# An attention and two-MoE kernel on one Trainium2 core: loads of v and of encoded weights in 64-row halves, k one slot sooner, decoding in other slots

## Chip, core and metric

The kernel runs on one core of one Trainium2 chip. The metric is the device time of one execution in microseconds (us). An execution with the profiler on gives the trace from which the rows below are read.

## The reference

For 4 batches, 12 heads, 448 tokens and 64 features per head the reference computes

```
scores = q @ k^T / 8                          (per batch and head, 448 x 448)
scores = sum over h of scores[h] * w_pre[h,g]
attn   = softmax(scores)
attn   = sum over h of attn[h] * w_post[h,g]
x      = attn @ v                             -> 1792 tokens x 768
x      = elu(x @ w_in) @ w_out                w_in 768 x 2048, w_out 2048 x 768
y      = top-1 mixture of 8 experts on x (768 -> 1024 -> 768, relu, gated)
```

w_in and w_out reach the kernel as 64-bit floats, seen as pairs of 32-bit words. The kernel makes 32-bit floats of them with a few integer steps, which it calls decoding.

## The kernel before

**Slots.** The attention stage walks through 16 chunks of queries (four per batch: 120, 120, 120 and 88 rows). A chunk is cut into units: six in each of the first three chunks of a batch, five in the last (four full ones and a half one). One unit is handled per *slot*; slots are numbered 0 to 91 in `S0`, 23 to a batch: 0 to 22, 23 to 45, 46 to 68, 69 to 91. The order of all instructions of all engines is written by hand: `at(slot, order, fn, ...)` files a call under a slot and a place in it, `half(y, ...)` under half slot y (slot y/2), and the calls run sorted by slot and order. The function `room` chooses between neighbouring half slots by a table of planned DVE and ACT costs.

**A unit.** The product of q and k (`qk`, L228) is copied from PSUM into the tile `st` by DVE and ACT (`qk_out`). Three slots ahead of a unit, `relayout` (L245) issues from POOL's queue the DMAs `sp<-st`, SBUF to SBUF, which bring the 12 heads of five queries into one column of partitions: four of 60 rows for a full unit. `premix` (L255) multiplies by w_pre, `rowmax` and `expo` (L261, L267) make the exponentials, `postmix` (L286) multiplies by w_post and the sums' reciprocals, `mt_out` (L304) copies the result. `av` (L332) multiplies by v once a chunk is complete, and `av_out` (L339, L340) sends the result to DRAM (`xscr`). The tile `sp` has 4 buffers, `ks` 9 (6 per batch), `raw` 2, `vt` 2.

**Loads.** All loads go from SP's queue, which takes them in the written order and stops at each that must wait:

- `load_q`: 192 KB, two per chunk. `load_k`: 224 KB, six per batch, for the next batch.
- `load_v` (L306 to L313): row blocks j = 0 to 3 of v at slots 1, 3, 5 and 7 of a batch (2, 4, 6 and 8 in batch 0). Blocks 0 to 2 are 128 rows of 3 KB in one DMA; block 3 has 64 rows, and they are loaded twice, into both halves of the partitions. In batch 0 each waits for a `premix` by `after(...)`.
- `dec_load` (L342): half a block of encoded weights, 128 rows of 3 KB.

**Decoding in the attention stage.** `dec_jobs` are three blocks of w_in and three of w_out, each in two halves: 12 half blocks. `spots` (L410) gives the slot of each one's first step: slots 10, 17 and 21 of batches 0 to 2, and slots 4, 8 and 13 of batch 3. The load is issued 5 half slots before. `dec_step` runs five DVE steps and one ACT step, and sends 128 rows of 1.5 KB of result to DRAM (`wscr`, `oscr`).

After the attention stage come the first MoE and the second one, which the change does not touch.

Of the kernel before, what the change touches and what calls it, by code (L numbers as in the profile page):

```python
# [8 lines left out]
U32 = mybir.dt.uint32  # L9
# [6 lines left out]
NB, H, S, D = 4, 12, 448, 64  # L16
# [84 lines left out]
def after(tc, ins, writes):  # L101
    for w in writes:
        tc.add_manual_dep(ins.ins, w.ins.name, mybir.DependencyInfo(mybir.DependencyClass.Sync, mybir.DependencyReason.DATA),
                          reason="rows of any scatter")
# [43 lines left out]
S0 = [0]  # L148
# [6 lines left out]
def attention(tc, pools, at, q, k, v, kron_pre, kron_post, dec_jobs, xscr):  # L155
# [3 lines left out]
    nc = tc.nc  # L159
    mm = nc.tensor.matmul  # L160
    sb = pools.open("a_sb", "right")
    early = pools.open("a_early", "left")
# [14 lines left out]
    dec = Decoder(nc, early, DM // 2, 2, 2, 2)  # L177

    ks, qs, qp, st, sp, pre, mxs, pt, sms, kpt, pst, mt, vt, avp, draw, dsteps, begun = ({} for _ in range(17))
# [5 lines left out]
    def values(b):  # L185
        vt[b] = sb.tile([128, 4, H, D], F32, name="vt", tag="vt", bufs=2)
# [116 lines left out]
        dst = mt[cc][:, :, 20 * g:20 * g + 2 * nr * T].rearrange("p x (w i) -> p w x i", i=T)  # L303
        nc.scalar.activation(dst, src, AF.Copy)  # L304

    def load_v(b, j):  # L306
        if j == 0 and b:
            values(b)
        n = min(128, S - 128 * j)
        for o in range(0, 128, n):  # L310
            ins = nc.sync.dma_start(vt[b][o:o + n, j], v[b, 128 * j:128 * j + n])
            if not b:
                after(tc, ins, [begun[divmod(1 + 2 * j, 6)]])  # L313

    def av(cc, a):

# [22 lines left out]
        nc.vector.tensor_copy(x[:, :, :n], avp.pop((cc, a))[:, :, :n])  # L339
        nc.sync.dma_start(xscr[b][:, 2 * a:2 * a + 2, o:o + n], x[:, :, :n])  # L340

    def dec_load(n, hf):  # L342
        draw[n, hf] = dec.load(dec_jobs[n][0], hf)

    def dec_step(n, hf, ix):
        if ix == 0:
            dsteps[n, hf] = dec.steps(draw.pop((n, hf)))
        fns, dst = dsteps[n, hf]
        fns[ix]()
        if ix == 5:  # L350
            nc.sync.dma_start(dec_jobs[n][1][:, hf * dec.width:(hf + 1) * dec.width], dst)
# [4 lines left out]
    def half(y, order, fn, *args):  # L356
        at(y / 2, order, fn, *args)
# [6 lines left out]
    def room(lo, hi, **cost):  # L364
        return take(min(range(lo, max(lo, hi) + 1), key=lambda y: max(use.get((e, y), 0) + c for e, c in cost.items())), **cost)

    def when(cc, u):

        if cc == 0:
            return 2 * ((2 * u + 1) * 10 // 12 - 13)  # L370
        lo, hi = S0[cc - 1] - 3, S0[cc] - 3
        return 2 * lo + u * (2 * hi - 2 * lo) // 6

    at(-100, 0, warm)
    for cc in range(NCH):
        z = S0[cc]
        for u in range(6):
            y = when(cc, u)
# [21 lines left out]
        half(y if soon else room(y + 1, y + 2, dve=35), 36, av_out, cc, a)  # L400
    for b in range(NB):
        for j in range(4):
            at(S0[4 * b] + 1 + 2 * j if b else 2 + 2 * j, 4, load_v, b, j)
        for u in range(6):
            half(when(4 * b, u) - 8 if b else 2 * (u - 20), 3, load_k, b, u)
    for cc in range(NCH):
        for u in range(2):
            half(when(cc, 3 * u) - 8 if cc else (-40, -36)[u], 3, load_q, cc, u)
    N = 2 * len(dec_jobs)
    spots = [S0[4 * b] + d for b in range(NB) for d in ((4, 8, 13) if b == NB - 1 else (10, 17, 21))]  # L410
    assert len(spots) == N
    first, free = 3, [0, 0]
    for i in range(N):
        n, hf = divmod(i, 2)
        z = max(first, free[i % 2], 2 * spots[i])
        first = y = room(z, z + 1, dve=85)
        half(y - 5, 3, dec_load, n, hf)
        half(y, 43, dec_step, n, hf, 0)
        half(y, 43, dec_step, n, hf, 2)
        y = room(y + 1, y + 2, act=61)  # L420
        half(y, 36, dec_step, n, hf, 1)
        y = room(y, y + 1, dve=57)
        half(y, 42, dec_step, n, hf, 3)
        y = room(y + 1, y + 2, dve=101)
        half(y, 43, dec_step, n, hf, 4)
        half(y, 43, dec_step, n, hf, 5)
        free[i % 2] = y + 1
# [934 lines left out]
def whole(tc, q, k, v, kron_pre, kron_post, w_in, w_out, w_gate, w1, w2,  # L1362
# [7 lines left out]
    with tc.tile_pool(name="dram", bufs=1, space=DRAM) as dr, tc.tile_pool(name="one", bufs=1, side="left") as one:  # L1370
# [17 lines left out]
        with tc.manual_schedule():  # L1388
            attention(tc, pools, at, q, k, v, kron_pre, kron_post,
                      [(src[f], to[f]) for src, to in ((w_in, wscr), (w_out, oscr)) for f in range(PRE)], xscr)  # L1390
            before, moe2_rest = moe2(tc, pools, w1, w2, ident, x2rows, R, out)
            moe1_rest = moe1(tc, pools, at, w_in, w_out, w_gate,
                             {"ident": ident, "tri": tri, "ones": ones, "em8": em8, "iota": iota, "tid": tid},
                             xscr, wscr, oscr, x2rows, R, before)
            for key in sorted(events):
                for fn, args in events[key]:
                    fn(*args)
            moe1_rest()
            moe2_rest()
# [61 lines left out]
```

## Time and profile before

| | |
|---|---|
| time before, median of 3 runs | 1202.42 us (1199.22 to 1205.14) |
| profiled execution, its own time | 1201.08 us |
| span of its trace (first to last instruction) | 1199.3 us |
| PE, DVE, ACT, POOL busy, share of the span | 96%, 64%, 57%, 25% |
| mean granted TensorE clock | 0.992 |

The time of the profiled execution is the span and 1.8 us around it. Engines: PE is TensorE's matmul, PEld its weight load, DVE VectorE, ACT ScalarE, POOL GpSimd, SP SyncE (it only issues DMAs here). An "idle before" is the time for which an engine stood idle just ahead of an instruction, with what ended it; "issue" is an engine that waited for nothing that the profile shows.

### The profile page before, as it was taken

What the parts mean: (1) busy time and instruction counts of PE and PEld (TensorE: products, weight loads), DVE (VectorE), ACT (ScalarE), POOL (GpSimd) and SP (SyncE); (2) the same over time, 40 slices, a digit from 0 to 9 for tenths busy, and PEclk for the clock granted to TensorE, in tenths of its full rate; (3) what the DMA queues carried; (4) which work ended last, traced back from release to release, by engine and by line L of the source; (5) the groups of instructions that cost most, each with busy time, mean ns of one, the idle gap of its engine ahead of it and who ended that gap; (6) DMA issues with size and microseconds to landing.
All of it is one profiled execution on the core that took longest, in us unless ns stands there. A gap on an engine that the chain in (4) does not pass through costs nothing.

```text
span 1199.3 us, 31078 instructions
## 1 busy us (share of the span) xinstructions
PE 1149.0 (96%) x12802; PEld 981.3 (82%) x12802; DVE 766.8 (64%) x1541; ACT 685.7 (57%) x1310; POOL 295.1 (25%) x466
## 2 busy tenths in 40 slices
PE   7989999899999999999999999999989999999995
PEld 3556666666667999999999987889779999999995
DVE  4667777667765878777777656555365655566662
ACT  4767777767776674645655344555434544455552
POOL 5656656546530003020211100000010110111110
PEclk9999999999999999999999999999999999999998
DMA  6997887888764428455573623334166665566551
GB/s 185 200 210 213 207 205 205 197 193 213 197 190 138 151 92 207 130 133 142 137 200 91 162 68 100 130 101 140 46 228 211 214 175 195 198 225 232 203 195 61
DMA packets 116444, 201.47 MB, mean 168 GB/s; under 512 B 45024, under 2 KB 76370, under 8 KB 116292
## 3 DMA queue, kind: packets, MB, share of 16 engines
q1 hardware_dynamic: 78116, 138.01, 37.1%
q0 software_dynamic: 38176, 61.37, 21.8%
q8 instruction: 103, 1.69, 0.6%
q14 instruction: 49, 0.40, 0.1%
HBM read 120.94 MB, written 30.09 MB: 126 GB/s over the span
## 4 chain that ended last, share of the span: by engine, by line
PE 85%; DMA 4%; ACT 3%; DVE 3%; issue 2%; POOL 1%; SPq 0%; POOLq 0%; ACTq 0%; DVEq 0%
PE p_h L533 14%; PE p_o L573 14%; PE p_h L1231 11%; PE p_z L1216 8%; PE p_post L286 7%; PE p_av L332 6%; PE p_qk L228 5%; PE p_pre L255 5%; PE acc L599 5%; PE p_o L533 4%; PE p_y L1231 3%; DMA sp<-st 3%; PE p_t L90 1%; POOL sp L245 1%; ACT mt L304 1%
## 5 line engine op out<-in xcount | busy, mean ns | idle before, releaser
L245 POOL DMA_DIRECT2D sp<-st x360 | 208.3, 593 | 135.4 <-PE p_pre L255 62.0
L267 ACT ACTIVATE pt<-p_pre,mx 128x448 f32<-128x448 f32 x180 | 112.9, 634 | 39.6 <-DVE mx L261 39.3
L286 PEld LDWEIGHTS p_post<-kp,pt 60*64 60x64 f32 (+1 forms) x5056 | 90.9, 135 | 43.7 <-ACT mt L304 26.3
L304 ACT ACTIVATE mt<-p_post 128x960 f32<-128x960 f32 (+1 forms) x92 | 101.6, 1104 | 42.1 <-PE p_post L286 42.0
L286 PE MATMUL p_post<-kp,pt 60*64 60x60 f32 (+2 forms) x5056 | 110.9, 229 | 11.3 <-issue 8.1
L261 DVE TENSOR_REDUCE mx<-p_pre 128x1 f32<-128x448 f32 x180 | 104.3, 619 | 23.2 <-PE p_pre L255 19.3
L590 POOL DMA_DIRECT2D x<-part x46 | 41.6, 928 | 291.5 <-ACT part L589 288.5
L1231 PE MATMUL p_h<-xgh,w1h 128*128 128x256 f32 (+1 forms) x384 | 109.6, 285 | 0.2 <-DVE h2l L1234 0.2
L1231 PE MATMUL p_h<-xgl,w1h 128*128 128x256 f32 (+1 forms) x384 | 109.3, 285 | 0.3 <-DVE xgl L1195 0.2
L1231 PE MATMUL p_h<-xgh,w1l 128*128 128x256 f32 (+1 forms) x384 | 109.3, 285 | 0.3 <-DVE w1l L112 0.3
L255 PE MATMUL p_pre<-sp,kpre 60*64 60x448 f32 x720 | 105.9, 540 | 3.3 <-DMA sp<-st 3.3
L573 PE MATMUL p_o<-gh,woh 128*128 128x448 f32 x288 | 106.4, 370 | 2.6 <-DVE x L586 2.6
L332 PEld LDWEIGHTS p_av<-mt,vt 128*64 128x64 f32 x1536 | 74.8, 137 | 38.9 <-issue 12.9
L573 PE MATMUL p_o<-gl,woh 128*128 128x448 f32 x288 | 105.2, 365 | 0.0
L573 PE MATMUL p_o<-gh,wol 128*128 128x448 f32 x288 | 104.9, 364 | 0.0
L228 PE MATMUL p_qk<-ks,qs 64*64 64x448 f32 x744 | 98.0, 541 | 5.0 <-ACT st L237 3.7
L235 DVE COPY st<-p_qk 128x448 f32<-128x448 f32 x93 | 57.9, 622 | 69.4 <-PE p_qk L228 56.3
L112 DVE TENSOR_TENSOR w2l<-w2raw,w2h 128x768 fp32r<-128x768 f32 (+1 forms) x60 | 60.7, 1012 | 51.4 <-ACT w2h L110 51.4
L332 PE MATMUL p_av<-mt,vt 128*64 128x120 f32 (+1 forms) x1536 | 85.6, 264 | 7.0 <-issue 5.1
L553 DVE SCALAR_TENSOR_TENSOR th<-rm,th 128x448 f32<-128x448 f32 x64 | 40.0, 625 | 80.6 <-ACT rm L552 80.6
L1267 POOL DMA_INDIRECT out_dram<-yrow,put x18 | 23.8, 1323 | 253.4 <-ACT w1h L110 86.7
L112 DVE TENSOR_TENSOR w1l<-w1raw,w1h 128x768 fp32r<-128x768 f32 x64 | 61.0, 960 | 28.2 <-ACT w1h L110 24.6
(199 smaller groups left out, 2811.6 us busy)
## 6 DMA issues: line engine op xcount, KB each, us to landing
sp<-st POOLq DMA_DIRECT2D x352, 105.0 KB
w1raw<-in_w_dram SPq DMA_DIRECT2D x64, 384.0 KB, 7.1
w2raw<-in_w_dram SPq DMA_DIRECT2D x48, 384.0 KB, 2.8
x<-part POOLq DMA_DIRECT2D x46, 224.0 KB
raw<-in_w_in_dram SPq DMA_DIRECT2D x13, 768.0 KB, 6.2
raw<-in_w_out_dram SPq DMA_DIRECT2D x13, 768.0 KB, 4.9
wtmp<-wscr SPq DMA_DIRECT2D x19, 384.0 KB, 3.9
wtmp<-oscr SPq DMA_DIRECT2D x19, 384.0 KB, 5.3
```

The lines of the kernel that those rows point to most:

```text
L112: nc.vector.tensor_tensor(l, src, a.bitcast(F32), ALU.subtract)
L228: mm(p[e][64 * a:64 * a + 64, :S], lhsT=qq[r, c:c + 64], rhs=kk[r], start=True, stop=True)
L245: nc.gpsimd.dma_start(t[64 * r:64 * r + 12 * T, c], st[cc][f:f + d * (T - 1) + 1:d])
L255: first = mm(ban[r][64 * c:64 * c + 64, :S], lhsT=kpre[x], rhs=t[x, c, :], start=True, stop=True)
L261: nc.vector.tensor_reduce(mxs[cc, g][:, r:r + 1], pre[cc, g][r][:, :S], AX.X, ALU.min)
L267: nc.scalar.activation(pt[cc, g][:, r], pre[cc, g][r][:, :S], AF.Exp, bias=mxs[cc, g][:, r:r + 1], scale=-1.0, accum_out=sms[cc, g][:, r:r ...
L286: mm(out, lhsT=e[x, r, 64 * s:64 * s + 64], rhs=kp[x, w].rearrange("p w (h i) -> p w h i", i=5)[:, :, :, :T], start=True, stop=True)
L304: nc.scalar.activation(dst, src, AF.Copy)
L332: mm(p[64 * e:64 * e + 64, u, :n], lhsT=vt[cc // 4][:, j, h, :], rhs=mt[cc][:, j * H + h, :n], start=(j == 0), stop=(j == 3))
L533: mm(p[:, :S], lhsT=a[:, c], rhs=m, start=(i == 0), stop=(i == 17))
L573: mm(p[:, :S], lhsT=a[:, c], rhs=m, start=(k == 0), stop=(k == 3 * len(fs) - 1))
L1231: mm(q[:, :N], lhsT=a[:, kk, :], rhs=m[:, kk, :], start=(j == 0), stop=(j == len(seq) - 1))
```

## The change

The loads of v become eight of 64 rows per batch, one per slot, in slots 0 to 7 of the batch (1 to 8 in batch 0, each behind the `premix` of the slot before). The loads of encoded half blocks become two of 64 rows, 6 and 5 half slots ahead of the decoding. k of the next batch is loaded two half slots (one slot) sooner. The 12 half blocks are decoded 2, 3, 3 and 4 per batch, not 3, 3, 3 and 3, in other slots.

```diff
-    def load_v(b, j):
-        if j == 0 and b:
+    def load_v(b, j, o):
+        if j == 0 and o == 0 and b:
             values(b)
-        n = min(128, S - 128 * j)
-        for o in range(0, 128, n):
-            ins = nc.sync.dma_start(vt[b][o:o + n, j], v[b, 128 * j:128 * j + n])
-            if not b:
-                after(tc, ins, [begun[divmod(1 + 2 * j, 6)]])
+        i = 128 * j + (o if j < 3 else 0)
+        ins = nc.sync.dma_start(vt[b][o:o + 64, j], v[b, i:i + 64])
+        if not b:
+            after(tc, ins, [begun[divmod(2 * j + o // 64, 6)]])
...
-    def dec_load(n, hf):
-        draw[n, hf] = dec.load(dec_jobs[n][0], hf)
+    def dec_load(n, hf, o):
+        w = 2 * dec.width
+        if o == 0:
+            draw[n, hf] = early.tile([128, w], U32, name="raw", tag="raw", bufs=2)
+        nc.sync.dma_start(draw[n, hf][o:o + 64], dec_jobs[n][0].bitcast(U32)[o:o + 64, hf * w:(hf + 1) * w])
...
         for j in range(4):
-            at(S0[4 * b] + 1 + 2 * j if b else 2 + 2 * j, 4, load_v, b, j)
+            for o in (0, 64):
+                at(S0[4 * b] + (0 if b else 1) + 2 * j + o // 64, 4, load_v, b, j, o)
         for u in range(6):
-            half(when(4 * b, u) - 8 if b else 2 * (u - 20), 3, load_k, b, u)
+            half(when(4 * b, u) - 10 if b else 2 * (u - 20), 3, load_k, b, u)
...
-    spots = [S0[4 * b] + d for b in range(NB) for d in ((4, 8, 13) if b == NB - 1 else (10, 17, 21))]
+    spots = [S0[4 * b] + d for b in range(NB) for d in ((3, 7, 11, 14) if b == NB - 1 else (11, 19, 22) if b else (19, 22))]
...
-        half(y - 5, 3, dec_load, n, hf)
+        half(y - 6, 3, dec_load, n, hf, 0)
+        half(y - 5, 3, dec_load, n, hf, 64)
```

## Rows read from the trace of the kernel before

**Rows 1.** The page: span, queue of instructions, chain that ended last.

```profile
span 1199.3 us, 31078 instructions
...
q8 instruction: 103, 1.69, 0.6%
...
PE 85%; DMA 4%; ACT 3%; DVE 3%; issue 2%; POOL 1%; SPq 0%; POOLq 0%; ACTq 0%; DVEq 0%
```

**Rows 2.** Windows of the attention, cut at slot starts: length, busy, clock, DMA, GB/s.

```profile
53.49:103.16 49.67, 46.34 (x1137) 31.59 (x1133) 36.15 (x96) 37.40 (x81) 31.29 (x55) 1.00 0.84 205
...
103.16:131.78 28.62, 28.62 (x717) 19.55 (x713) 20.43 (x57) 22.20 (x50) 19.28 (x34) 1.00 0.82 216
131.78:142.86 11.08, 10.32 (x252) 7.36 (x248) 6.89 (x18) 7.55 (x17) 5.93 (x11) 1.00 0.85 192
142.86:188.44 45.58, 43.41 (x1064) 29.70 (x1062) 33.91 (x92) 35.33 (x77) 26.91 (x48) 1.00 0.86 205
...
216.74:230.29 13.55, 10.41 (x252) 7.32 (x248) 6.89 (x18) 7.71 (x17) 6.72 (x12) 1.00 0.70 167
230.29:277.69 47.40, 44.76 (x1064) 30.75 (x1062) 34.04 (x92) 35.35 (x77) 26.80 (x48) 0.96 0.82 197
277.69:331.42 53.73, 49.91 (x1245) 34.52 (x1240) 39.73 (x108) 40.10 (x88) 33.52 (x59) 1.00 0.84 209
```

**Rows 3.** PE's timeline, first product of slots 43, 44 and 45: start, us.

```profile
179.12 0.98 PE L255 MATMUL p_pre<-sp,kpre 60*64 60x448 f32 x8
...
181.53 1.06 PE L255 MATMUL p_pre<-sp,kpre 60*64 60x448 f32 x8
...
186.03 0.97 PE L255 MATMUL p_pre<-sp,kpre 48*64 48x448 f32 x4
```

**Rows 4.** Windows with the DMA engines full, columns as in Rows 2.

```profile
154.29:166.00 11.71, 10.91 (x262) 7.04 (x258) 7.99 (x21) 8.56 (x20) 8.09 (x15) 1.00 1.07 232
...
237.23:252.31 15.08, 14.09 (x356) 9.41 (x352) 10.72 (x29) 11.13 (x25) 9.21 (x17) 1.00 1.06 234
300.00:310.00 10.00, 8.34 (x207) 5.41 (x197) 6.10 (x16) 6.81 (x14) 4.82 (x9) 1.00 1.04 252
30.00:53.00 23.00, 21.38 (x474) 13.07 (x469) 14.69 (x39) 17.46 (x38) 14.11 (x26) 1.00 1.00 203
```

**Rows 5.** PE's timeline in slot 54: the longest idle time.

```profile
220.76 0.55 PE L286 MATMUL p_post<-kp,pt 60*64 60x60 f32 x14 [2.41 <-issue]
```

**Rows 6.** Waits from 20 to 350 us: us in total, times, longest.

```profile
PEld p_pre L255 <- DMA sp<-st: 10.3, 24, 2.1
...
PE p_post L286 <- issue: 8.1, 6, 2.4
...
PE p_av L332 <- issue: 5.1, 4, 1.7
```

**Rows 7.** DMA issues: count, KB each, median us from issue to landing.

```profile
sp<-st POOLq DMA_DIRECT2D x352, 105.0 KB
...
qs<-in_q_dram SPq DMA_DIRECT2D x32, 192.0 KB, 5.2
...
ks<-in_k_dram SPq DMA_DIRECT2D x24, 224.0 KB, 7.9
...
xscr<-xc SPq DMA_DIRECT2D x36, 120.0 KB, 4.2
...
raw<-in_w_in_dram SPq DMA_DIRECT2D x6, 384.0 KB, 7.7
...
vt<-in_v_dram SPq DMA_DIRECT2D x8, 192.0 KB, 6.0
```

**Rows 8.** Timeline of SP's queue, slot 38: start and length of issue.

```profile
157.26 0.59 SPq L201 DMA_DIRECT2D ks<-in_k_dram  x1
157.91 2.04 SPq L127 DMA_DIRECT2D raw<-in_w_in_dram  x1
```

**Rows 9.** Groups by line, 20 to 350 us: a decoding step of DVE.

```profile
L142 DVE SCALAR_TENSOR_TENSOR dec_p<-raw,dec_p 128x384 uint32<-128x384 uint32 x12 | 6.6, 550 | 0.0
```

More of the change, by code (lines that the diff above doesn't have):

```diff
@@ L340, in av_out @@
         nc.sync.dma_start(xscr[b][:, 2 * a:2 * a + 2, o:o + n], x[:, :, :n])
-    def dec_load(n, hf):
-        draw[n, hf] = dec.load(dec_jobs[n][0], hf)
+    def dec_load(n, hf, o):
[3 more added lines that the diff above has]
+        nc.sync.dma_start(draw[n, hf][o:o + 64], dec_jobs[n][0].bitcast(U32)[o:o + 64, hf * w:(hf + 1) * w])
     def dec_step(n, hf, ix):
         if ix == 0:
-            dsteps[n, hf] = dec.steps(draw.pop((n, hf)))
+            dsteps[n, hf] = dec.steps(draw.pop((n, hf)).rearrange("p (c w) -> p c w", w=2))
         fns, dst = dsteps[n, hf]
```

## The prediction, made before the changed kernel was built or run

> **What bounds the kernel now.** I read the page first: the chain that ended last is 85% PE and 4% DMA [rows 1], so what PE loses in the attention stage is lost at the end, as far as PE follows behind without a gap. Then PE's timeline: where nothing disturbs it, the first products of slots 43 and 45 are 6.91 us apart, 2.41 us for the first slot of such a pair and 4.50 us for the second [rows 3]. That is 3.455 us a slot, with PE busy throughout.
>
> Next I cut the stage at slot starts [rows 2]. Slots 23 to 30 take 28.62 us with PE busy for all of them: the eight slots with the loads of v cost nothing, and serve as floor for such eight. All else is held against the pairs:
>
> - Batch 0 from slot 10 on (13 slots): 49.67 us against 6 x 6.91 + 2.41 = 43.9, so 5.8 us lost.
> - Batch 1, slots 31 to 33: 11.08 against 2 x 2.41 + 4.50 = 9.3, 1.8 lost. Slots 34 to 45: 45.58 against 6 x 6.91 = 41.5, 4.1 lost.
> - Batch 2, the same two stretches: 13.55 and 47.40, so 4.2 and 5.9 lost. (In the second the clock is 0.96 on the mean, a short fall behind the stall.)
> - Batch 3, slots 69 to 82: 53.73 against 28.6 + 3 x 6.91 = 49.3, 4.4 lost.
>
> Together 26.2 us. Where PE loses, the DMA engines are full: share of 1.04 to 1.07 at 232 to 252 GB/s [rows 4]. There PE stops in the middle of a run of like products, for nothing that the profile shows, up to 2.41 us [rows 5]; 13.2 us in postmix and av [rows 6]. PE's weight loads wait 10.3 us for `sp<-st` [rows 6]. Both fit a full set of DMA engines: relayouts late, and, I think, PE's own instructions late, which come by a DMA queue of their own (103 packets, 1.69 MB [rows 1]).
>
> **What fills the engines.** A slot's bytes from the code and the sizes [rows 7], in KB of 1024 bytes: four relayouts 420; per chunk two q of 192 and three `xscr` of 120; k 224, half a v block 192, an encoded half block 384, its result 192. The full stretches carry about 235 GB/s (232 and 234 in the two long windows, 252 in the short one [rows 4]), which is 229.5 KB per us or 793 KB per slot. I sum each slot's excess over 793 (a shortfall works it off, not below zero) and take the peak as us of backlog:
>
> - Before, 31 starts the load of a half block behind v: slots 30 and 31 carry 804 and 1084, peak 302 KB, 1.3 us; lost 1.8 and 4.2 (batches 1, 2), mean 3.0.
> - Before, k with the next half block: slots 34 to 39 carry 1060, 956, 836, 764, 1028, 732 (SP issues the last k and the half block within 0.7 us [rows 8]); peak 679 KB, 3.0 us; lost 5.8, 4.1 and 5.9 (batches 0, 1, 2), mean 5.3.
> - Before, batch 3: slots 70 to 76 carry 924, 1116, 804, 508, 996, 1084, 804; peak 685 KB, 3.0 us; lost 4.4.
> - Before, a peak of 0.9 us at slot 28 lost nothing.
>
> **The change part by part.**
>
> *Half blocks away from v and k.* With the new spots and `room`'s choice they load at slots 16, 17, 19, 20 of batch 0; 31, 32, 39, 40, 42, 43 of batch 1 and likewise in batch 2; 69, 70, 73, 74, 77, 78, 80, 81 of batch 3, 192 KB each. *k a slot sooner* ends at slot 37, before the half block of 39. New peaks:
>
> - Batch 0, k alone (988, 836, 764, 836, 764): 252 KB, 1.1 us. Between 0.9 (nothing) and 1.3 (3.0 us); I take 1.0, since the lumps inside a slot are halved too. Bounds 0 and 3.0.
> - Batches 1 and 2, v at slots 24, 25 (924, 924): 262 KB, 1.1 us: again 1.0 each.
> - Batches 1 and 2, k with one result (988, 836, 764, 1028, 764): 444 KB, 1.9 us. On the line from 0.9 and 0 to 3.0 and 5.3 it loses 2.5, between 1.3 and 3.0 us of peak 3.8; I take their mean, 3.2, each.
> - Batch 3 (slots 69 to 74: 804, 1116, 924, 612, 892, 1188): 778 KB, 3.4 us, higher than before: 4.4 becomes 4.9 (upper bound 6.6, by half as much again).
>
> Left: 1.0 + 2 x (1.0 + 3.2) + 4.9 = 14.3; gain 26.2 - 14.3 = 11.9 us.
>
> *Start of batch 0.* No half block loads beside v before slot 9. 393 kB at the 203 GB/s of that stretch [rows 4] are 1.9 us; the last piece of v still waits for the premix of slot 7. I take 1.5, bounds 0 and 1.9. With v one slot sooner, the q loads at slots 2, 5 and 8 stand behind premixes 0, 3 and 6; each is used four slots later, so this costs nothing; without that cover qk would wait for q's 5.2 us [rows 7].
>
> *More DMAs.* 24 more on SP's queue (12 for v, 12 for half blocks), 0.6 us each [rows 8], 14 us over the stage: nothing on the path, hidden behind SP's waits for the chunk results that it sends (`xscr`). If that cover were gone, k and q would go out 0.6 us later per piece ahead of them. The engines' time for a half piece: the two halves of block 3 land in 6.0 us, a whole half block in 7.7 [rows 7]; and the window with the most GB/s, 252, is one with both halves of v in it [rows 4]. I cost a piece by its bytes, nothing extra; from below a gain has no reason; upper bound a whole one's time, in the rivals.
>
> [...]
>
> *Decoding.* Five DVE steps of 0.55 us at most [rows 9] and one ACT step per half block, as many as before. The one added in batch 3 ends a slot later (85 for 84), 2.8 us of DVE at most, beside PE; priced at nothing, bounds 0 and 2.8. Its result is read only in the first MoE. k's buffers are free six half slots before they are written, so no new wait.
>
> **Sum.** 1201.1 - 11.9 - 1.5 = 1187.7, say 1188 us. The profiled execution lies 1.3 us under the median of the runs, so the gain against that is 14 us. Bounds of this case: all at the dear end (3.0 + 2 x (3.0 + 3.8) + 6.6 + 2.8 = 26.0 lost, start 0) 1200.9; all at the cheap end (2 x 2.5 + 4.4 = 9.4 lost, start 1.9) 1182.4.
>
> **Rivals.**
>
> *The smoothing does it all.* If the lumps inside a slot, not the sum over slots, make PE stop, batches 0 to 2 lose nothing: 21.8 and the start's 1.5 gained, 1178. For it: 0.9 us of peak is free, and the stops follow within a few us of whole blocks [rows 5, 8]. Against: k's stretch stays over 793 KB per slot.
>
> *A 64-row piece costs as much as a 128-row one* (other side). Each half piece then takes 0.84 us more. Slots 69 to 82 carry 11040 KB, 48.1 us, and 16 pieces add 13.4: 61.5 where they took 53.7, so 7.8 lost. Batches 1 and 2 become bound by DMA: 16896 KB, 73.6 us, 14 pieces 11.8, and 1.8 that slots 41 to 45 can't fill: 87.2 against 85.3 and 89.3 now, together -0.2. Batch 0 keeps 3.8 of its 4.8; its start gains 1.9 and pays for six pieces, 5.0. Sum 7.8 - 0.2 - 3.8 + 3.1 = +6.9: 1208. It decides from a piece at 1.7 times its bytes on (13.4 gained at 1, 6.9 lost at 2). Against it stand the landing times and the 252 GB/s above.
>
> *PE's stops are not the loads'.* "issue" names no transfer; if PE's instructions come late by themselves, moving loads moves only the relayouts' waits, and the rest comes back elsewhere: 1199, no change. For it: the waits that I read name no load of v or of weights [rows 6]. Against: slots 23 to 30, full of the same instructions, have no stop. [...]
>
> **How the numbers follow.** Forecast 0.52, smoothing does it all 0.22, no change 0.16, dear pieces 0.10. Range 1178 to 1200 leaves out some 0.07 below and 0.13 above; the likeliest case alone spans 1182 to 1201. 0.5% (6 us) is about what a measurement of this kernel can tell from no change: the forecast case lies below 1196.4 for 0.50 of its 0.52, so faster 0.72. Of the dear pieces, on the edge at 1208, 0.07 count as slower, with 0.02 of the no-change case: slower 0.09, same 0.19.
>
> **What would show it.** Right: slots 31 to 33 and 54 to 56 back to 9.3 us; batch 0 from slot 10 near 45 us; batches 1 and 2 near 83.6 us from first slot to first slot; PE's "issue" idle halved; batch 3 no better than 53.7. Wrong: windows with v in them with a DMA share above 1 at under 210 GB/s (dear pieces); "issue" unchanged at another place (rival 3); the decoding at slots 83 to 85 on the chain.

## The result, and the profile after

The change made the kernel slower: 1215.42 us median (1206.83 to 1218.88, six runs) against 1200.82 us before (six runs on the same chip), a ratio of 1.0114, 95% interval 1.0073 to 1.0156. The profiled execution took 1218.88 us with a span of 1217.1 us, 17.8 us over that of before.

The page of the changed kernel: span, the instruction queue, the chain that ended last.

```profile
span 1217.1 us, 31120 instructions
...
q8 instruction: 103, 1.69, 0.6%
...
PE 84%; DMA 5%; ACT 3%; issue 3%; DVE 2%; POOL 1%; SPq 0%; POOLq 0%; DVEq 0%; ACTq 0%
```

"issue" grew from 2% to 3% and DMA from 4% to 5% of the chain [rows 1]. The windows of the changed kernel, cut where those of before were, with slots 0 to 9 and 46 to 53 added; columns as in [rows 2]:

```profile
16.20:57.26 41.06, 35.01 (x643) 21.58 (x638) 23.09 (x57) 26.67 (x58) 25.58 (x45) 1.00 1.01 185
57.26:104.25 46.99, 45.94 (x1137) 31.71 (x1140) 33.37 (x89) 35.59 (x78) 30.12 (x54) 1.00 0.82 198
104.25:136.90 32.65, 30.06 (x717) 20.94 (x713) 21.03 (x59) 22.73 (x51) 19.57 (x35) 0.95 0.93 195
136.90:148.83 11.93, 10.16 (x252) 6.95 (x246) 6.74 (x17) 7.32 (x17) 5.60 (x10) 1.00 1.06 194
148.83:196.44 47.61, 43.58 (x1066) 29.71 (x1063) 33.65 (x91) 35.04 (x78) 26.70 (x48) 1.00 0.74 188
196.44:230.99 34.55, 31.19 (x716) 21.56 (x712) 21.19 (x59) 22.80 (x51) 19.58 (x35) 0.90 0.90 189
230.99:242.08 11.09, 10.18 (x253) 6.70 (x246) 6.74 (x17) 7.32 (x17) 5.63 (x10) 1.00 1.07 192
242.08:289.23 47.15, 44.15 (x1064) 29.86 (x1062) 33.56 (x91) 35.05 (x78) 26.69 (x48) 1.00 0.75 191
289.23:348.56 59.33, 52.77 (x1245) 36.06 (x1241) 41.82 (x113) 41.30 (x90) 33.59 (x58) 0.97 0.89 199
```

Two windows of before were not shown yet, slots 0 to 9 and 46 to 53:

```profile
17.42:53.49 36.07, 32.03 (x645) 19.61 (x643) 22.89 (x57) 25.63 (x58) 24.61 (x44) 1.00 0.91 199
188.44:216.74 28.30, 28.30 (x717) 19.40 (x713) 20.45 (x57) 22.21 (x50) 18.52 (x34) 1.00 0.83 213
```

Line by line: slots 0 to 9 went from 36.07 to 41.06 us, slots 10 to 22 from 49.67 to 46.99, slots 23 to 30 from 28.62 to 32.65, slots 34 to 45 from 45.58 to 47.61, slots 46 to 53 from 28.30 to 34.55, batch 3's slots 69 to 82 from 53.73 to 59.33. The four stretches that carry v (0 to 9, 23 to 30, 46 to 53, 69 to 82) lost 5.0, 4.0, 6.3 and 5.6 us. Of the stretches that the change was to mend, 10 to 22 and 54 to 56 gained 2.7 and 2.5 and 57 to 68 gained 0.3; 31 to 33 and 34 to 45 lost 0.9 and 2.0. Three windows of the changed kernel in which loads of v are under way (in the first with two of k):

```profile
45.00:57.00 12.00, 8.15 (x180) 5.49 (x172) 4.85 (x13) 7.00 (x15) 6.29 (x12) 1.00 1.04 185
119.00:130.00 11.00, 8.41 (x188) 5.67 (x182) 4.69 (x13) 6.65 (x13) 4.82 (x9) 0.88 1.08 197
212.00:223.00 11.00, 7.64 (x179) 5.17 (x175) 4.67 (x13) 5.89 (x13) 4.61 (x8) 0.85 1.05 201
```

These are the windows that the prediction named as the mark of dear pieces: DMA share above 1, v among the loads, and 185 to 201 GB/s where full windows of before carried 203 to 252 [rows 4]. PE's waits (from 20 to 370 us) and the landing times:

```profile
PE p_post L286 <- issue: 17.7, 8, 3.4
...
PEld p_pre L255 <- DMA sp<-st: 7.8, 26, 1.3
```

```profile
vt<-in_v_dram SPq DMA_DIRECT2D x32, 192.0 KB, 8.6
...
ks<-in_k_dram SPq DMA_DIRECT2D x24, 224.0 KB, 9.3
```

PE's stops without a releaser in postmix doubled, from 8.1 to 17.7 us [rows 6]; over all lines, those over 0.5 us rose from 13.6 to 24.2 us. The relayouts' own lateness (10.3 us to 7.8) did not grow. The landing times are weak evidence: 8.6 us for a 192 KB piece of v against 6.0, and 9.3 us for k against 7.9 [rows 7], are medians of the few loads whose landing the profile tells, 3 of 32 against 2 of 8 and 1 of 24 against 2. The two longest stops, in PE's timeline (slot 8 and slot 51), stand in the middle of a run of like products:

```profile
50.83 0.49 PE L286 MATMUL p_post<-kp,pt 60*64 60x60 f32 x13 [3.44 <-issue]
...
220.59 1.12 PE L286 MATMUL p_post<-kp,pt 60*64 60x60 f32 x23 [3.36 <-issue]
```

### The profile page after: what moved, and what is told of

Read it like the earlier page. It is cut to its first block, busy times and chain, and to the rows that moved or that the text cites. A ratio compares the mean times of both kernels' runs of the same rounds, so it can differ in the third digit from the quotient of the medians.

```text
span 1217.1 us, 31120 instructions
## 1 busy us (share of the span) xinstructions
PE 1159.4 (95%) x12802; PEld 988.6 (81%) x12802; DVE 767.2 (63%) x1541; ACT 685.5 (56%) x1310; POOL 294.4 (24%) x466
## 4 chain that ended last, share of the span: by engine, by line
PE 84%; DMA 5%; ACT 3%; issue 3%; DVE 2%; POOL 1%; SPq 0%; POOLq 0%; DVEq 0%; ACTq 0%
PE p_h L537 14%; PE p_o L577 13%; PE p_h L1235 11%; PE p_z L1220 8%; PE p_post L286 7%; PE p_av L331 5%; PE p_qk L228 5%; PE p_pre L255 5%; PE acc L603 5%; PE p_o L537 4%; DMA sp<-st 3%; PE p_y L1235 3%; POOL sp L245 1%; PE p_t L90 1%; PE tp L90 1%
## 5 line engine op out<-in xcount | busy, mean ns | idle before, releaser
L286 PEld LDWEIGHTS p_post<-kp,pt 60*64 60x64 f32 (+1 forms) x5056 | 95.2, 137 | 52.0 <-issue 26.3
L286 PE MATMUL p_post<-kp,pt 60*64 60x60 f32 (+2 forms) x5056 | 115.4, 231 | 21.3 <-issue 17.7
L255 PE MATMUL p_pre<-sp,kpre 60*64 60x448 f32 x720 | 114.4, 553 | 3.5 <-DMA sp<-st 1.6
L228 PE MATMUL p_qk<-ks,qs 64*64 64x448 f32 x744 | 103.9, 554 | 9.0 <-ACT st L237 5.1
L331 PE MATMUL p_av<-mt,vt 128*64 128x120 f32 (+1 forms) x1536 | 83.6, 262 | 2.5 <-ACT mt L304 1.5
```

The lines of the kernel that those rows point to most:

```text
L228: mm(p[e][64 * a:64 * a + 64, :S], lhsT=qq[r, c:c + 64], rhs=kk[r], start=True, stop=True)
L255: first = mm(ban[r][64 * c:64 * c + 64, :S], lhsT=kpre[x], rhs=t[x, c, :], start=True, stop=True)
L286: mm(out, lhsT=e[x, r, 64 * s:64 * s + 64], rhs=kp[x, w].rearrange("p w (h i) -> p w h i", i=5)[:, :, :, :T], start=True, stop=True)
L331: mm(p[64 * e:64 * e + 64, u, :n], lhsT=vt[cc // 4][:, j, h, :], rhs=mt[cc][:, j * H + h, :n], start=(j == 0), stop=(j == 3))
```

## The experiments

Ratios are against the kernel before on the same chip, with 95% intervals. A stretch of one profile is worth less than a ratio: batch 3's slots 69 to 82, whose work is ordered alike in before, e8, e9 and e13, took 53.73, 54.84, 56.37 and 57.59 us in their single profiles.

**e1_whole: the change with whole loads.** All new places kept, each pair of halves loaded as one 128-row piece at the place of the first half (v) or the second (half blocks).

```diff
-        i = 128 * j + (o if j < 3 else 0)
-        ins = nc.sync.dma_start(vt[b][o:o + 64, j], v[b, i:i + 64])
+        if j < 3 and o:
+            return
+        n = 128 if j < 3 else 64
+        i = 128 * j
+        ins = nc.sync.dma_start(vt[b][o:o + n, j], v[b, i:i + n])
...
```

> The changed kernel's schedule (spots, k a slot sooner, v from slot 0 on), but v's blocks 0 to 2 and the encoded half blocks in whole loads of 128 rows again, at the place of the first piece of v and of the second piece of a half block. Theory A, pieces of 64 neighbouring rows cost the DMA engines about as much as 128 rows: with whole loads the forecast's case holds, 1185 to 1197 us. Theory B, the new schedule itself is worse (v earlier, k earlier, four half blocks in batch 3): stays at 1210 to 1217. Theory C, more DMAs and semaphores on SP's queue cost it: 1185 to 1197 as A.

1.0049 [1.002, 1.0078], 1203.08 us, between the two theories. More than half of the loss is gone with the halves, but not all of it: the schedule costs something too.

**e2_striped, e3_columns: as many pieces, cut another way.** Even and odd rows (first), or left and right columns (second), in place of upper and lower 64 rows; half blocks likewise; block 3 of v keeps its two halves.

```diff
-        i = 128 * j + (o if j < 3 else 0)
-        ins = nc.sync.dma_start(vt[b][o:o + 64, j], v[b, i:i + 64])
+        if j < 3:
+            i = 128 * j + o // 64
+            ins = nc.sync.dma_start(vt[b][o // 64:128:2, j], v[b, i:i + 127:2])
...
```

```diff
+        if j < 3:
+            h = slice(0, 6) if o == 0 else slice(6, 12)
+            ins = nc.sync.dma_start(vt[b][:, j, h], v[b, 128 * j:128 * j + 128, h])
...
```

> The changed kernel with the same number of pieces at the same places, each of 64 rows of 3 KB, but the even rows and the odd rows instead of the lower and the upper half (block 3 of v keeps its two halves). Theory A (what is dear is that the 64 rows lie side by side in one half of the partitions): 1185 to 1198 us, windows with v in them at 215 GB/s and more. Theory B (schedule) and theory C (number of DMAs): 1210 to 1218, windows with v at 185 to 201 GB/s as in the changed kernel.

> The changed kernel with the same number of pieces at the same places, each over all 128 rows but half the columns (1.5 KB a row, 128 packets for 64; block 3 of v keeps its two halves). Theory A: 1185 to 1200 us, a little above e2 if the shorter packets cost something. Theories B and C: 1210 to 1218.

1.0033 [1.0004, 1.0062] and 1.0057 [1.0035, 1.0079]: both like whole loads (1.0049), not like the halves (1.0114), though they have the change's 24 more DMAs and its order. So it is not the number of pieces that costs, nor SP's time to issue them, but that a piece is 64 neighbouring rows. The gain that theory A expected (1185 to 1200 us) did not come: the medians are 1202.53 and 1204.28 us. With many landings told, they do not set the cuts apart: a 192 KB piece of v lands after 7.1 us as even or odd rows, 6.8 as columns and 7.3 as a half (e4).

**e4_v_only: the kernel before, with v alone as the change has it** (halves, new slots).

> The kernel before with v alone loaded as in the change: eight pieces of 64 rows, one per slot from slot 0 (1 in batch 0); half blocks whole, spots and k as before. Theory A: v's stretches become dear as in the changed kernel, slots 23 to 30 take 31 to 33 us for 28.6, the start of batch 0 some 5 us longer: 1212 to 1222 us. Theory B: 1196 to 1204. Theory C: 1201 to 1208 (12 more DMAs of the 24).

1.0112 [1.0062, 1.0162], four runs: v alone makes as large a loss as the whole change. Half blocks in halves, their new slots and the earlier k add nothing that can be measured, though by the two intervals they could be worth some 0.6% either way. e1 to e4 ran on one chip: 1208.63 us with halves of v is 4 to 6 us over e1, e2 and e3.

The DMA packets of the traces show the cost row by row. A packet of 3,072 bytes (mostly a row of v or of a half block) took 180 ns at the mean between the first and the last slot of before, 182 in e1, 195 in e2, 211 in e4 and 224 in the changed kernel.

**e6_spots, e8_k: the new decoding slots alone, k a slot sooner alone.** One line each of the change's diff.

> The kernel before with the new spots of the decoding alone (2, 3, 3 and 4 half blocks per batch); v, k and whole loads as before. If the half blocks beside v and k are what PE loses by, as I forecast: ratio 0.992 to 0.997 (start of batch 0 1.5 us, slots 10 to 22 3 us, slots 34 to 45 and 57 to 68 1.6 and 3.4 us shorter, batch 3 up to 1 us longer). If the spots themselves cost (four half blocks in batch 3): 1.000 to 1.004.

> The kernel before with k loaded one slot sooner alone. Theory E: the first two loads of k now stand ahead of the first chunk result on SP's queue, go out some 10 us sooner, and meet v's last blocks: slots 0 to 9 take 37.5 to 39 us for 36.1, ratio 1.000 to 1.004. If k sooner helps as forecast: 0.996 to 1.000, slots 0 to 9 unchanged.

1.000 [0.997, 1.003] and 0.9995 [0.997, 1.0019]. k a slot sooner neither helped nor cost (slots 0 to 9 took 35.99 us, not the 37.5 to 39 of theory E). The new decoding slots did what was forecast in k's stretches of batches 1 and 2, and gave it back elsewhere. Windows of e6_spots: slots 10 to 22, 34 to 45, 46 to 53, 57 to 68, 69 to 82.

```profile
52.16:101.37 49.21, 47.03 (x1134) 31.98 (x1137) 33.48 (x89) 36.00 (x79) 30.38 (x54) 1.00 0.83 198
140.54:184.49 43.95, 42.91 (x1066) 29.37 (x1063) 33.32 (x90) 34.86 (x76) 26.58 (x48) 1.00 0.86 211
184.49:214.44 29.95, 28.82 (x717) 19.86 (x713) 20.99 (x59) 22.52 (x51) 19.48 (x35) 1.00 0.89 209
228.27:272.26 43.99, 42.94 (x1065) 29.55 (x1062) 33.34 (x90) 34.86 (x76) 26.69 (x48) 1.00 0.85 210
272.26:328.59 56.33, 51.47 (x1244) 35.34 (x1240) 41.53 (x113) 41.12 (x90) 33.66 (x59) 0.97 0.89 210
```

45.58 and 47.40 us became 43.95 and 43.99 [rows 2]; slots 46 to 53 rose from 28.30 to 29.95 and batch 3 from 53.73 to 56.33. Slots 10 to 22, where 3 us were expected, went from 49.67 to 49.21. 43.95 and 43.99 are also the shortest, within 0.1 us, that any run showed, and the same trace tells why. Its windows of slot 38 and of slot 40, and of the q and k products (L228) in slots 38, 40 and 44:

```profile
154.38:160.14 5.76, 4.72 (x109) 3.07 (x106) 3.42 (x11) 3.82 (x10) 3.70 (x7) 1.00 1.06 228
162.55:168.26 5.71, 5.71 (x122) 3.86 (x117) 3.33 (x11) 4.40 (x11) 3.53 (x7) 1.00 0.90 223
```

```profile
154.38:160.14 5.76, 1.21 (x12) 0.21 (x8) 1.00 1.06 228
...
162.55:168.26 5.71, 2.28 (x16) 0.90 (x16) 1.00 0.90 223
177.58:182.07 4.49, 0.98 (x12) 0.30 (x8) 1.00 0.73 177
```

Slot 40 holds 16 products of q and k, 2.28 us, where the undisturbed slot 44 has 0.98 us of them: PE is busy for all of its 5.71 us, 1.22 more than slot 44's 4.49 [rows 3]. Slot 38 stands 1.04 us still, for ACT's copy of the scores, in this trace, and 0.76 to 1.05 us in all fifteen of full kernels:

```profile
156.48 0.98 PE L228 MATMUL p_qk<-ks,qs 64*64 64x448 f32 x8 [1.04 <-ACT st L237]
```

So slots 34 to 45 come to 41.5 + 1.22 + 1.27 = 44.0 us, not to 6 x 6.91 = 41.5. The 1.22 is PE's own work; that the wait in slot 38 (5.76 - 4.49 = 1.27) could never go is not shown, as e11 has none in slot 61, its like in batch 2.

**e7_paced: the even and odd rows, each load of v, of k and of half blocks held until the premix of the slot before its own has begun.**

```diff
+    def paced(ins, s):
+        x = -int(-s // 1) - 1
+        cc = max(c for c in range(NCH) if S0[c] <= x)
+        after(tc, ins, [begun[cc, x - S0[cc]]])
...
```

> As e2 (even and odd rows, changed schedule), with a wait added to every load of v, of k for the next batch and of half blocks: it goes out only once PE has made the premix product of the slot before its own. Theory D, SP issues the pieces in bunches, two or three together, each time that a chunk result lets its queue go, so that they are not spread at all: with the waits slots 23 to 30 come down to 28.6 to 29 us and the ratio to 0.988 to 0.997. If bunches are not it: 1.001 to 1.006 as e2; above 1.006 if the waits hold up q or the chunk results behind them.

0.9995 [0.997, 1.0021] against 1.0033 [1.0004, 1.0062] without the wait: perhaps better, the intervals overlap. Slots 23 to 30 took 30.10 us, not the 28.6 to 29 of theory D, so that bunches are not shown to be what they lose by. It was tried because in the changed kernel the pieces did not go out one per slot. SP's timeline there, 110 to 130 us:

```profile
113.03 0.93 SPq L206 DMA_DIRECT2D qs<-in_q_dram  x1
114.42 0.48 SPq L310 DMA_DIRECT2D vt<-in_v_dram  x1
115.01 0.52 SPq L339 DMA_DIRECT2D xscr<-xc  x1
115.59 2.96 SPq L310 DMA_DIRECT2D vt<-in_v_dram  x2
121.99 0.38 SPq L339 DMA_DIRECT2D xscr<-xc  x1
122.46 0.45 SPq L206 DMA_DIRECT2D qs<-in_q_dram  x1
122.96 1.54 SPq L310 DMA_DIRECT2D vt<-in_v_dram  x2
```

Here SP stands still from 118.55 us on, until DVE's copy of a chunk's result ends at 121.96 and `xscr` can go, and then sends by 124.50 a load of q and two pieces of v that were written behind it. Two halves filed under two slots so left together, as a whole block would, only in two pieces, which the bench (e12) shows 0.16 us dearer each beside relayouts.

**e5_alone, e12_bench: the loads by themselves.** No attention and no MoE. In e5_alone the stages ran into each other, so that it tells the ways apart only roughly; e12_bench is the same, with rows of v in place of encoded weights and stages that wait for each other.

> No attention and no MoE: the kernel only loads the same 24 encoded half blocks (9.4 MB) eight times over, whole, as lower and upper halves, as even and odd rows, and as left and right columns, each way once alone and once beside 64 of the relayouts sp<-st; relayouts alone stand first; the output is zeros. Theory A (64 neighbouring rows are dear): alone the halves take 1.3 to 2 times as long as the whole loads; even and odd rows and columns take at most 1.1 times. Beside the relayouts the same order, halves at under 210 GB/s. If only the count of DMAs is dear (theory C), the three ways in pieces take the same, longer than whole. If pieces are dear only beside the relayouts, the four ways are alike alone and part beside them.

> The loads by themselves, no attention and no MoE (the output is zeros): nine stages one after the other, each ended by a read of all tiles before the next begins. Each stage loads 24 blocks of 128 x 3 KB (9.4 MB) whole, or in halves of 64 neighbouring rows, or in even and odd rows, or in left and right columns; each way alone and beside 64 relayouts of 60 rows (6.9 MB); and the relayouts alone. Theory (a piece of 64 neighbouring rows is dearer than its bytes): halves take 1.2 to 2 times the time of whole blocks, even and odd rows at most 1.1 times, beside the relayouts and alone. Rival (a piece costs its bytes, and what the pieces cost in the kernel is their number or their place): the four ways within 5% of each other.

e5_alone, 458.46 us, gave no clean stage. e12_bench (591.38 us), windows from a stage's first issue to its last landing: whole, alone and beside relayouts; halves, the same; even and odd rows; columns. Columns: length, DVE, POOL, clock, DMA share, GB/s.

```profile
91.89:118.90 27.01, 22.96 (x69) 0.00 (x0) 1.00 0.93 349
120.80:192.97 72.17, 18.50 (x32) 36.70 (x64) 1.00 0.92 227
204.69:246.39 41.70, 23.60 (x73) 0.00 (x0) 1.00 0.98 227
247.62:327.36 79.74, 18.52 (x32) 36.70 (x64) 1.00 0.99 205
339.24:373.21 33.97, 23.59 (x73) 0.00 (x0) 1.00 0.84 278
374.45:445.50 71.05, 18.42 (x32) 36.70 (x64) 1.00 0.98 230
457.20:485.72 28.52, 23.73 (x74) 0.00 (x0) 1.00 0.96 331
486.74:558.88 72.14, 18.71 (x33) 36.68 (x64) 1.00 1.04 236
```

Alone, 24 blocks take 27.01 us whole and 41.70 in halves: 1.54 times, with the engines busy for 0.98 of the time. (41.70 - 27.01) / 48 is 0.31 us more for each half piece. Columns cost 1.06 times, even and odd rows 1.26. Beside relayouts the halves add 79.74 - 72.17 = 7.6 us, 0.16 us a piece, and the two other cuts nothing. The packets agree: a row of 3,072 bytes takes 130 ns whole, 208 in halves and 146 as even or odd rows, and beside relayouts 196, 234 and 199. The theory held for halves alone. Beside relayouts they made 1.10 times, under its 1.2, and even and odd rows alone missed the 1.1.

**e9_late, e15_late_all: half blocks decoded at the end of each batch.** Whole loads in their old places; slots 19, 21 and 23 of batches 0 to 2, and in e15 slots 8, 12 and 15 of batch 3 as well.

```diff
-    spots = [S0[4 * b] + d for b in range(NB) for d in ((4, 8, 13) if b == NB - 1 else (10, 17, 21))]
+    spots = [S0[4 * b] + d for b in range(NB) for d in ((4, 8, 13) if b == NB - 1 else (19, 21, 23))]
```

> The kernel before, and only the slots in which half blocks are decoded changed: slots 19, 21 and 23 of batches 0 to 2 (all loads whole, k and v where they were), batch 3 as before. Theory (a stretch loses what comes in late blocks of instructions and late relayouts behind a full set of DMA engines, over a floor that counts the slots with two products of q and k; the new slots alone reached that floor in slots 34 to 45 and 57 to 69 and gave it back in slots 46 to 53 and in batch 3): with batch 3 left as it was, slots 34 to 45 near 44 us (45.6 before) and slots 57 to 68 near 44 us (47.4 before), batch 3 at 53.7, and a ratio of 0.991 to 0.997. Rival (the DMA engines have the same bytes to carry and a load moved away only stops PE elsewhere): ratio 0.998 to 1.003, what slots 34 to 45 gain coming back in slots 46 to 56 and 69 to 71.

> The kernel before with the decoding in slots 19, 21 and 23 of batches 0 to 2, as in the run with late slots, and in slots 8, 12 and 15 of batch 3 in place of 4, 8 and 13; all loads whole and in their old places. Theory (a half block is cheap where no k and no v is loaded; in batch 3 v is loaded in slots 70 to 76 and nothing later): slots 69 to 82 near 52 us in place of 53.7 to 56.4, ratio 0.991 to 0.996, a little under the 0.996 of the run with late slots. Rival (the decoding that ends later is then in the way of the last slots, or batch 3 loses to v alone): slots 69 to 90 no shorter than 82 us together, ratio 0.996 to 1.000.

e9_late is a little faster than the kernel before: 1194.42 us against 1198.77, 0.9959 [0.9933, 0.9985]. Slots 57 to 68 came to 44.57 us as expected, slots 34 to 45 (45.79) did not. e15_late_all, 0.9976 [0.9953, 0.9998], is no better; its slots 69 to 82 took 56.44 us, not the 52 expected, so that moving batch 3's half blocks showed no gain.

**e10_v_slots, e13_v_batch0, e14_v_batches123: whole blocks of v a slot sooner,** everywhere, in batch 0 alone, in batches 1 to 3 alone.

```diff
-            at(S0[4 * b] + 1 + 2 * j if b else 2 + 2 * j, 4, load_v, b, j)
+            at(S0[4 * b] + (0 if b else 1) + 2 * j, 4, load_v, b, j)
...
```

> The kernel before, and only v a slot sooner: whole blocks of 128 rows, each one slot ahead of its old place in every batch, with the wait for the premix of the slot before in batch 0. Theory (the new slots of v cost something whatever the size of a piece: they put v into slot 0, where the last half block, the last values and the first q of the batch still are): slots 0 to 9 near 38 us (36.1 before, 38.1 with the whole schedule and whole loads), ratio 1.002 to 1.006. Rival (the size of the piece alone is what v costs, the place is free): slots 0 to 9 at 36 us, slots 23 to 30 at 28.6, ratio 0.998 to 1.002.

> The kernel before, and v a slot sooner in batch 0 alone (whole blocks). Theory (what v's new slots cost lies in the first ten slots, where relayouts have only 2 to 7 us of lead and v now meets the first q): slots 0 to 9 near 40 us (36.1 before, 40.3 with v sooner in all batches), ratio 1.002 to 1.005, as much as in all batches together (1.0035). Rival (the cost is spread over the batches): ratio 1.000 to 1.001, slots 0 to 9 at 36 to 37.

> The kernel before, and v a slot sooner in batches 1 to 3 alone (whole blocks), batch 0 as before. Theory (the cost lies in batch 0): ratio 0.998 to 1.001, slots 0 to 9 at 36 us, slots 23 to 30 and 46 to 53 at most 1 us over 28.6 and 28.3. Rival (in batches 1 to 3 the first block of v now stands right behind the result of the last half block and the values of the batch before, and the full stretch starts a slot earlier): slots 23 to 30 and 46 to 53 at 30 to 32 us as with v sooner in all batches, ratio 1.002 to 1.004.

1.0035 [1.0005, 1.0065], 1.0014 [0.999, 1.0039] and 1.0027 [0.9999, 1.0054]. The place costs something by itself; how it divides over the batches the two last runs do not settle. In batch 0 one place of the cost is plain. PE's timeline in slot 8 of e13_v_batch0:

```profile
51.95 0.68 PE L286 MATMUL p_post<-kp,pt 60*64 60x60 f32 x13 [4.64 <-issue]
```

PE stops ahead of the same matmul, the 597th, in all eight kernels that load v sooner in batch 0 (1.84 to 4.64 us; 3.44 in the changed kernel). Of the seven that load it in the old slots, six have no stop over 0.5 us there and e6_spots one of 0.55.

Part of that comes back at once. The window of slots 10 to 22 in e13_v_batch0, to be held against 49.67 us before and 49.21 in e6:

```profile
59.22:106.42 47.20, 45.64 (x1136) 30.95 (x1132) 35.97 (x96) 37.09 (x81) 27.80 (x49) 1.00 0.86 202
```

The eight kernels with v sooner in batch 0 take 46.3 to 48.4 us for these slots, the other seven 48.2 to 49.9. So the 2.7 us that the changed kernel gained there came mostly with v, not with the half blocks.

**e11_burst: four idle loads of 384 KB at slots 20, 43 and 66 of the kernel before,** into tiles that nothing reads.

```diff
+    def burst():
+        for i in range(4):
+            t = early.tile([128, DM], F32, name="idler", tag="idler", bufs=3)
+            nc.sync.dma_start(t, v[0, :128])
+    for z in (20, 43, 66):
+        at(z, 2, burst)
```

> The kernel before with four more loads of 384 KB each at slots 20, 43 and 66, into tiles that nothing reads. Theory (PE's stops with no releaser are blocks of its instructions that come late when the DMA engines are full): behind each burst PE stops 1 to 3 us at the next place where the count of its instructions is 192 to 193 over a multiple of 256, in stretches that had no stop before, and nowhere else with that mark; about 1.5 MB at 235 GB/s are 6.7 us of transfers, so the attention stage grows by 4 to 12 us in all. Rival (PE's stops come from PE or its operands): no new stop marked issue near the bursts, only waits for relayouts.

1210.28 us in one run. Windows of slots 23 to 30 and 46 to 53, and PE's timeline at slot 46:

```profile
100.83:134.19 33.36, 29.20 (x716) 19.66 (x715) 20.81 (x57) 22.27 (x50) 20.66 (x36) 1.00 0.95 222
189.99:223.99 34.00, 30.39 (x717) 20.96 (x716) 20.52 (x58) 22.15 (x50) 19.05 (x34) 0.95 0.86 209
```

```profile
189.99 0.54 PE L255 MATMUL p_pre<-sp,kpre 60*64 60x448 f32 x1
194.14 0.98 PE L255 MATMUL p_pre<-sp,kpre 60*64 60x448 f32 x7 [3.61 <-issue]
```

Both stretches were without a stop before; here slots 46 to 53 have one of 3.61 us with nothing to release it, one product into a premix. New stops came, as the theory said, this one longer than its 3 us; it is one run and one profile. Where such stops fall was counted in all fifteen traces of full kernels: the number of instructions that PE's queue had issued (weight loads, matmuls, semaphore steps) when PE stopped "issue" for over 0.5 us between 20 and 400 us.

```
kernel             stops   count mod 256 = 192   = 193   other
before                10                     5       5       0
after                 14                     8       6       0
burst                 15                     6       9       0
twelve others        114                    53      61       0
```

The packets of the instruction queue q8, of 16,384 bytes each, keep step with this count. At each of the 153 stops, as many packets had ended as PE had passed such places before, and the last had ended 1.2 to 2.0 us before PE went on. At the 805 such places that PE passed without a stop over 0.5 us, it had mostly ended sooner (2.6 us at the median). The DMA share in the 4 us up to that packet's end was 0.9 or more at 139 of the 153 stops, and at 265 of the 805: full engines are where the stops are, but they do not always make one.

## Why the prediction was wrong, step by step

**The kernel is bound by PE, and PE loses to full DMA engines: right, by the counts and by e11.** "I think, PE's own instructions late" agrees with the counts: all 153 stops fall at the same two neighbouring counts modulo 256, each behind a packet of q8 that had ended 1.2 to 2.0 us before PE went on (2.6 us at the median where PE did not stop), and idle loads alone make new ones (15 stops in e11 for 10 before). The sizes agree too: PE's queue issues 25,872 instructions in the kernel before and q8 brings 103 packets of 16.4 kB [rows 1], 251 instructions to a packet on the mean, near the 256 of the count. So a stop is taken here for a wait for the next packet; that is inferred from the counts, and no row shows the wait itself. Of the 958 such places 805 were passed without a stop over 0.5 us. Ahead of 139 of the 153 stops the DMA share was 0.9 or more, and the stops came to 17.7 us in postmix alone in the changed kernel.

**"26.2 us lost", held against 6.91 us a pair: mis-sized, by about two.** The shortest that any of the fifteen traces shows is 46.35 us for slots 10 to 22, 10.54 and 10.71 for 31 to 33 and 54 to 56, 43.92 and 43.97 for 34 to 45 and 57 to 68, and before's own 53.7 for 69 to 82: 11.8 us under before in all, and no kernel reaches them together. A pair is no floor where a slot holds two groups of q and k products (slot 40: 5.71 us of PE busy) or waits for ACT (slot 38). 9.3 us was never seen in slots 31 to 33.

**"I cost a piece by its bytes, nothing extra": failed, and this is the greater part.** The second rival was right in kind. Halves against whole in the same places are 1.0114 against 1.0049, and for v alone 1.0112 (e4) against 1.0035 (e10): 8 to 9 us; on the one chip of e1 to e4 it is 4 to 6. Its price was too high: 0.84 us was put on a piece, and the bench shows 0.31 alone and 0.16 beside relayouts. 24 pieces of v at 0.31 would be 7.4 us, an estimate that has every one of them on PE's path; the 24 pieces of half blocks cost nothing that shows (e4 against the change), so a price by the piece does not give the whole. The measured loss of 14.6 us is over the 6.9 of the rival's sum; the next two points, which it did not have, go the same way, but no run divides the rest. The two facts that spoke against it misled: the stretch of 252 GB/s held two halves of v's block 3, but they are 393 of its 2,520 kB, and the landing of two halves (6.0 us) was set beside that of a single half block (7.7 us) that has twice their bytes. The bench agrees with the rival in direction (alone, 64 neighbouring rows 1.54 times the whole loads, left and right columns 1.06 times) and not in size, as a half piece at a whole one's time would make it 2 times. Even and odd rows, 64 to a piece as well, took 1.26 times alone and nothing extra beside relayouts. Why neighbouring rows are the dear ones, no run here shows.

**"Start of batch 0", 1.5 us gained: the wrong sign.** Slots 0 to 9 took 41.06 us for 36.07. The step counted the bytes that left the stretch and not when the rest would go: with v a slot sooner PE stops in slot 8, for 3.44 us here and for 1.84 to 4.64 us in every kernel that has v so in batch 0 (e10: 2.57, e13: 4.64, with whole blocks). Slots 10 to 22 then give part of it back. Over the whole kernel the new slots of v cost 1.0035; how much of it falls outside batch 0 is open.

**"Half blocks away from v and k", -11.9 us: right in k's stretches of batches 1 and 2, nothing in sum.** There e6 gained 5.0 us where the sum had 3.6 (10.0 lost, 2 x 3.2 left), and gave it back in slots 46 to 53 and, within what single profiles vary, in batch 3. In slots 10 to 22 the sum had 4.8 us and e6 gained 0.5; slots 54 to 56 took 13.83 us in e6 (13.55 before) but 11.10 in e13, which changes nothing behind batch 0, so that their 11.09 in the changed kernel can't be put down to the half blocks. Byte sums per slot took it for granted that a DMA goes out in the slot under which it is filed; where the changed kernel's SP queue was read, it sent the pieces in bunches behind `xscr`. That this is why the sum failed is argued, not shown (e7). With old v and whole loads the same idea, put nearer to the end of a batch, gained 0.4% (e9).

**k sooner, 24 more DMAs, decoding: nothing, as said.** e8 0.9995; e2 and e3 carry the 24 DMAs at no measurable price beyond e1.

**The third rival (the stops are not the loads')** fell with e11, though its neutral result is what e6 and e8 measured: where only places change, the stops move.

Of the marks named ahead: slots 31 to 33 and 54 to 56 went to 11.93 and 11.09, not 9.3; batch 0 from slot 10 to 46.99, not 45; batches 1 and 2 from first slot to first to 92.2 and 92.8 (196.44 - 104.25 and 289.23 - 196.44), not 83.6; PE's stops marked "issue" rose to 1.8 times (13.6 to 24.2 us) in place of halving; batch 3 did not get better. The mark against, windows with v under 210 GB/s at a share above 1, is there.

## What to carry to other kernels

When a load is to be made finer, try its columns or every other row first, not its partitions in neighbouring halves (1.06, 1.26 and 1.54 times the whole loads alone in e12; 1.00, 0.98 and 1.10 beside relayouts), and look whether the queue that sends the pieces stands still in between: two pieces of v that stood behind the same `xscr` were issued here in 1.54 us (122.96 to 124.50). A loss in PE marked "issue" can be counted: if its stops fall at one place of a fixed count, as all 153 here at 192 or 193 modulo 256, a load that fills the DMA engines at that moment can be on PE's path, though no tile of it is waited for (e11: 3.61 us at slot 46, with loads that nothing reads). Take a floor from the slots themselves, with what PE has to do in each, before calling the rest a loss.

## What the runs showed of the hardware beyond that

The stop of 3.36 us in slot 51 of the changed kernel cost PE twice, as idle time and by a lower clock behind it. Windows of 2 us around it:

```profile
218.00:220.00 2.00, 0.00 (x0) 0.00 (x0) 0.00 (x0) 0.00 (x0) 1.77 (x4) 0.90 1.07 222
220.00:222.00 2.00, 1.41 (x27) 1.15 (x31) 0.00 (x0) 0.24 (x1) 0.34 (x2) 0.50 1.06 191
...
224.00:226.00 2.00, 2.00 (x58) 1.65 (x56) 1.27 (x3) 0.55 (x2) 0.91 (x2) 0.50 0.05 16
226.00:228.00 2.00, 2.00 (x28) 0.98 (x22) 1.31 (x5) 2.00 (x6) 1.39 (x3) 0.89 0.50 126
```

The granted clock falls from 1.00 to 0.50 while PE stands still, and stays there until about 226 us. Slots 46 to 53 have PE busy for 31.19 us where the same matmuls took 28.30 before: 2.9 us on top of the stop. The longer stop of slot 8 (3.44 us) had a clock of 1.00 behind it, so that not each stop does this. Over the nine windows of the stage PE's busy time rose by 8.9 us (294.1 to 303.0), about half of the loss; the rest is idle time (9.4 us), no more than the stops grew by (10.7 us). Not all of the 8.9 us is at a lower clock: in slots 0 to 9 PE's busy time rose by 3.0 us at a clock of 1.00. Single products there are as long as before (premix 547 ns for 545, postmix 229 for 229), so that they overlap less; why, no run here shows.
